# Adding the input in memory: output tiles turned into staging and accumulated by GpSimd's transfers, in a linear-attention and MLP block

## The chip, the cores and the metric

The kernel runs on one core of a Trainium2 chip, with one launch. The metric is the device time of one execution in microseconds; lower is better. Where several runs are shown, their median is used. Engines are called by their names: TensorE (PE, with its weight loads as PEld), VectorE (DVE), ScalarE (ACT), GpSimd (POOL) and SyncE (SP). SP, ACT and GpSimd can all issue DMA transfers, which run on the core's sixteen DMA engines.

## The reference

One input `x` of 2048 tokens by 512 features in float32 is normalised, and two blocks run on the same normalised tokens. Both are added to `x`:

```
xn  = layernorm(x)                       # no scale or bias
qkv = xn @ wqkv                          # 512 x 1536, 32 heads of 16
q, k = phi(q), phi(k)                    # phi(t) = (t+1 if t > 0 else exp(t)) + 1e-6
kv  = sum over tokens of k^T v,  z = sum over tokens of k
A   = ((q kv) / (q z + 1e-6)) @ wo       # 512 x 512
B   = relu(xn @ w1 + b1)^2 @ w2 + b2     # 512 x 1376, 1376 x 512
out = x + A + B
```

The last line is the one that matters here: the input, untouched, is added to the sum of both blocks before it is stored.

## The kernel before

**How the work is tiled.** The 2048 tokens are four blocks of 512 (`BT`); a block's result is held feature-major, so an output tile is 128 features by 512 tokens, and there are four of them per block (`TB = 4`), sixteen in all. Every float32 product is made of three passes over a rounded high part and a low part of each operand. The products of two token blocks at a time are done with Strassen's scheme, seven products for eight.

**Stages.** First, sixteen token tiles of 128 are loaded, normalised, transposed (the first eight by TensorE, the others by VectorE after thirty-two small transfers `xg<-xp` that regroup them) and multiplied by the key weights; the key-value sums grow on TensorE (`kx`). Behind the loop over tiles the values and the fused matrix of `wo` are made (`values`, `matrix`). Then a loop `for n in range(2)` handles two token blocks each: blocks t1 and t2 are 3 and 2 in the first pass, 1 and 0 in the second. A pass has an inner loop over pairs of weight columns `p` (two pairs for the attention's queries, seven for the MLP), whose results are kept in `rr` tiles, and then a list of jobs that multiply the squared or normalised rows with `w2` and the fused matrix. Operand tiles `ops` of the weights are spilled to memory (`wd`) in the first pass and loaded again later; eight buffers of them rotate.

**How an output tile leaves.** The result of a job stands in PSUM (`acc`, `ps`) or, in the second pass, partly in SBUF (`m1`, `m5`, `u2`), features by tokens. `add_turned` transposes it on VectorE in blocks of 32 by 32 into a scratch tile `o` and adds it with a second VectorE instruction to a staging tile `res`, which `load_res` has filled with the same block of `x` earlier: eight transfers of 128 KB, each for 32 partitions and with runs of 256 bytes. `store` writes the staging tile to the output in transfers of the same shape. The second half of the features of block t2 in the second pass is stored by SP and ACT in turn, and the very last tile is turned, added and stored in two parts (`PARTS`, `flush`).

**What sets the order.** The whole kernel is recorded first. `Program.add` collects the instructions with what they read and write; `Program.order` then gives every one a due time and plays the program up to 150 times with costs from `cost`, shifting due times where TensorE had to wait in the play, and keeps the best order. TensorE's own order is as recorded; the others (DVE, ACT, GpSimd, SP) take, at each moment, the ready instruction that is due first. The resulting instructions are emitted in that order, each engine's list is fixed, and an engine executes its list strictly in order. All profile rows of these instructions therefore carry one line, L301 (`emit`), and are told apart by tile names. A tile's buffer is named by its tag: `res` of the first pass takes the buffers `r3` (t1) and `r0` (t2), and in the second pass `slots_of` gives `r3` to the `rr` tile of pair 0 and `r0` to that of pair 5. The output tensor is kept out of the recorder's dependencies (`apart`), as nothing reads it. Transfers take one of eight semaphores in turn for SP and ACT together, so that each of them waits for the one eight before it; GpSimd's transfers have eight of their own.

L1568 reserves room for descriptors of GpSimd's transfers: `dynamic_dma_scratch_size=1024`, in bytes per partition. In the kernel before GpSimd issues no transfer.

Of the kernel before, what the change touches and what calls it, by code (L numbers as in the profile page):

```python
# [10 lines left out]
OP = mybir.AluOpType  # L11
# [63 lines left out]
class Program:  # L75
# [7 lines left out]
    def __init__(self, nc):  # L83
        self.nc = nc
        self.tasks = []
        self.seen = {}
        self.fixed = 0
        self.apart = None
        for e in ("tensor", "vector", "scalar", "gpsimd", "sync"):
            setattr(self, e, Recorder(self, e))  # L90
# [13 lines left out]
    def add(self, engine, name, args, kw):  # L104
# [7 lines left out]
        outs = [r for r in outs if r[0] != self.apart]  # L112
        t.preds, t.first = {}, []
        for regions, write in ((ins, False), (outs, True)):
            for r in regions:
                before = self.seen.get(r[0], [])
                hit = [(o, wrote) for q, o, wrote in before
                       if (write or wrote) and q[0] < r[2] and r[1] < q[1] and q[2] < r[4] and r[3] < q[3]]
                if isinstance(r[0], Place) and r[0].last and not hit:
                    t.first.append(r[0].last)  # L120
                for o, wrote in hit:
                    if o is not t:
                        t.preds[o.index] = max(t.preds.get(o.index, 0), 1 if wrote else 0)
# [11 lines left out]
    def cost(self, t, out, ins):  # L135
# [16 lines left out]
        elif t.engine == "vector":  # L152
            a, b = self.DVE.get(t.name, (0.1, 0.5))
            t.dur = a + src * b / 960
            t.lock = t.name in ("tensor_tensor", "scalar_tensor_tensor") and n > 64 and not any(map(in_psum, ins))
        elif t.engine == "gpsimd":
            t.dur = 0.2 + src * 2.3 / 1000 if t.name == "tensor_tensor" else 0.3
            t.lock = t.name == "tensor_tensor"
        else:
            b = 1  # L160
            for s, k in out.ap:
                b *= k
            run = 1
            for a in (out, *ins):
                d = list(a.ap)
                c = d[-1][1] if d[-1][0] == 1 else 1
                run = min(run, c) if run > 1 else c
            t.size, t.lag = 4 * b, 2.8 if b > P * P else 2.0
            t.dur = 0.43 if out.ap[0][1] == P and run >= 512 else 0.62 if ins and isinstance(ins[0], View) and isinstance(out, View) else 0.5
            t.size = t.size * max(1.0, (0.009 + run * 4 / 27e3) / (run * 4 / 24e3)) if run > 1 else b * 150  # L170
# [142 lines left out]
def kernel(  # L313
# [831 lines left out]
    for i in range(2, NT):  # L1145
# [29 lines left out]
        if i == 3:  # L1175
            advance()
        if i == 8:
            run(*[lambda j=j: piece_v(j) for j in range(NJ)])
# [66 lines left out]

    def load_res(t, pool, tag):
        r = pool.tile([P, 2, BT // 32, 64], F32, name=f"res{t}", tag=tag)
        for g, h, rows in out_blocks(xf, t):
            nc.sync.dma_start(r[g, h], rows)
        return r  # L1250

    def add_turned(r, c, src, part=slice(0, BT)):
# [5 lines left out]

    def store(r, t, *halves, by=None, blocks=slice(0, BT // 32)):
        for g, h, rows in out_blocks(of, t):  # L1260
            if h in halves:
                (by or nc.sync if g.start % 64 else nc.sync).dma_start(rows[:, blocks], r[g, h, blocks])

# [9 lines left out]
    for n in range(2):  # L1273
# [75 lines left out]
        for p in range(NK + 1):  # L1349
# [61 lines left out]
            if n == 0 and p == NK - 1:  # L1411
                res = {t1: load_res(t1, work, "r3")}

# [11 lines left out]
        if n == 0:  # L1425
# [8 lines left out]
            sums = sums_of(xT[t1 - 2], xT[t2 - 2])  # L1434
            outs = [lambda c=c: add_turned(res[t1], c, acc[c]) for c in range(TB)]
            outs.append(lambda: store(res[t1], t1, 0, 1))

            made_t = []

            def step(e):  # L1440
                if e == 10:
                    res[t2] = load_res(t2, work, "r0")
                if e > 5:
# [35 lines left out]
            for c in range(TB):  # L1479
                add_turned(res[t2], c, acc_2[c])  # L1480
            store(res[t2], t2, 0, 1)
            continue

        X, Z = acc[:2], acc[2:]
        res = {t1: load_res(t1, keep, "B0"), t2: load_res(t2, keep, "A0")}
        W, Y = ([bank(f"{u}{c}", loop_tag) for c in range(2)] for u in "WY")
# [13 lines left out]
        def turned_to(t, a, src):  # L1500
            for c in range(2):
                add_turned(res[t], a + c, src[c])

# [24 lines left out]
        jobs.append((lambda: hz[:, 0], lambda s: second_z([*Z, *Y], range(NJ), s)))  # L1528
        at_end(lambda: (add_to(o["m1"], Z), turned_to(t1, 0, o["m1"])))
        jobs += phase_jobs(X, 5)  # L1530
# [3 lines left out]
        jobs += phase_jobs(X, 6)  # L1534
        at_end(lambda: (add_to(o["m5"], X), turned_to(t2, 2, o["m5"]), store(res[t2], t2, 1, by=nc.scalar)))
        jobs += phase_jobs(Y, 3, False, True)
        at_end(lambda: (add_to(o["u2"], Y), turned_to(t1, 2, o["u2"]), store(res[t1], t1, 0, 1)))
        jobs.append((lambda: hz[:, 1], lambda s: second_z(X, range(2), s)))
# [3 lines left out]
        def flush(part):  # L1542
            add_turned(res[t2], 1, ends_in[part.start], part)
            store(res[t2], t2, 0, by=nc.scalar, blocks=slice(part.start // 32, part.stop // 32))

# [36 lines left out]
```

## Time and profile before

| | us |
|---|---|
| three runs | 410.43, 410.69, 410.69; median 410.69 |
| the profiled execution | 410.82 |
| its span, from the first to the last instruction | 409.1 |
| TensorE busy in it | 402.0 |
| VectorE busy in it | 338.8 |
| ScalarE busy in it | 264.4 |
| GpSimd busy in it | 28.3 |
| granted TensorE clock, mean | 0.997 |

The page gives the busy time of each engine, the span in forty slices, and the chain of work that ended last, followed back from the last instruction. The groups of instructions name output tile and input tile (`res<-o,res` is the add of a turned tile into staging), partitions by elements, a count, then busy time, the mean of one in ns and the idle time of the engine just before them with what ended it. The rows of DMA issues end with the median time from the issue to the landing of the data. A timeline row has the start, the duration, the engine and the instruction, with the idle time before it and what released it in brackets. A row of windows gives, for a stretch, its length, the busy time of PE, PEld, DVE, ACT and POOL with counts, the granted clock, the busy share of the DMA engines and GB/s.

### The profile page before, as it was taken

Reading aid. Unit: us, or ns where it says so; the run is one execution under the profiler, and the core shown is the slowest. Engines: PE = TensorE matmul, PEld = TensorE weight load, DVE = VectorE, ACT = ScalarE, POOL = GpSimd, SP = SyncE. Lnnn points to the kernel's source line nnn. Section 1 sums busy time; section 2 is a strip of 40 time slices with the busy share of each in tenths; the row PEclk is TensorE's granted clock in tenths of the full one; section 3 lists DMA queues with packets and bytes.
Section 4 is the critical chain, followed back from the end, with each engine's and each line's share of the span. In section 5 each row is a group of like instructions: output and inputs, shape, how many; then the busy total and the mean of one; then the engine's idle time right before and its main releaser. Section 6 shows DMA issues by size and latency. Waiting matters only on the chain.

```text
span 409.1 us, 5570 instructions
## 1 busy us (share of the span) xinstructions
PE 402.0 (98%) x1805; PEld 333.1 (81%) x1805; DVE 338.8 (83%) x578; ACT 264.4 (65%) x449; POOL 28.3 (7%) x48
## 2 busy tenths in 40 slices
PE   8999999999999999999999999999999999999994
PEld 7788888888888888888888888888888888888883
DVE  5899997989788699999989742799999999786794
ACT  5786666766867988889952421367888777545430
POOL 2233422220000000000000000000000000000000
PEclk9999999999999999999999999999999999999998
DMA  7863524933979779756799999999877789979424
GB/s 241 279 169 96 163 70 108 334 107 116 358 272 322 245 271 316 270 217 260 269 336 279 292 378 359 273 297 377 282 238 254 269 220 269 266 250 279 159 52 103
DMA packets 80497, 99.34 MB, mean 243 GB/s; under 512 B 40306, under 2 KB 51570, under 8 KB 80212
## 3 DMA queue, kind: packets, MB, share of 16 engines
q1 hardware_dynamic: 78324, 98.47, 75.0%
q10 hardware_dynamic: 2144, 0.52, 0.6%
q8 instruction: 14, 0.23, 0.2%
q14 instruction: 15, 0.12, 0.1%
HBM read 60.96 MB, written 35.92 MB: 237 GB/s over the span
## 4 chain that ended last, share of the span: by engine, by line
PE 98%; DVE 1%; ACT 0%; issue 0%
PE ps L301 53%; PE acc L301 44%; DVE res L301 0%; DVE o L301 0%; ACT xs1h L301 0%; DVE zb L301 0%; DVE odds L301 0%
## 5 line engine op out<-in xcount | busy, mean ns | idle before, releaser
L301 PE MATMUL ps<-s,ops 128*128 128x512 f32 x393 | 91.5, 389 | 0.0
L301 PEld LDWEIGHTS ps<-s,ops 128*128 128x128 f32 x393 | 73.8, 188 | 15.3
L301 PE MATMUL acc<-s,ops 128*128 128x512 f32 (+1 forms) x294 | 67.1, 382 | 0.0
L301 PEld LDWEIGHTS acc<-s,ops 128*128 128x128 f32 x294 | 54.1, 188 | 10.8
L301 PE MATMUL acc<-pk,tok 128*128 128x512 f32 x192 | 47.1, 394 | 0.0
L301 ACT ACTIVATE s<-rr 128x512 fp32r<-128x512 f32 x50 | 31.3, 632 | 21.7 <-DVE s L301 10.9
L301 PEld LDWEIGHTS acc<-pk,tok 128*128 128x128 f32 x192 | 35.4, 188 | 7.9 <-DVE pk L301 0.6
L301 DVE TENSOR_TENSOR s<-rr,s 128x512 fp32r<-128x512 f32 x50 | 34.1, 688 | 9.3 <-ACT s L301 8.2
L301 PE MATMUL ps<-T,ops 128*128 128x512 f32 x168 | 41.4, 390 | 0.0
L301 PE MATMUL acc<-T,ops 128*128 128x512 f32 x168 | 41.2, 389 | 0.0
L301 PEld LDWEIGHTS acc<-T,ops 128*128 128x128 f32 x168 | 31.5, 188 | 6.5
L301 PEld LDWEIGHTS ps<-T,ops 128*128 128x128 f32 x168 | 31.5, 188 | 6.5
L301 POOL TENSOR_TENSOR tok<-xp,tok 128x512 fp32r<-128x512 f32 x16 | 23.1, 1443 | 41.9 <-ACT tok L301 24.1
L301 PE MATMUL ps<-xs0h,ops 128*128 128x512 f32 x72 | 23.7, 389 | 0.0
L301 ACT ACTIVATE ops<-raw 128x512 fp32r<-128x512 f32 (+1 forms) x28 | 16.2, 591 | 4.3 <-PE ps L301 2.1
L301 DVE TENSOR_TENSOR ops<-raw,ops 128x512 fp32r<-128x512 f32 (+1 forms) x28 | 17.1, 617 | 1.6 <-ACT ops L301 1.5
L301 PE MATMUL acc<-xs0h,ops 128*128 128x512 f32 x56 | 18.4, 389 | 0.0
L301 ACT ACTIVATE s<-rf 128x512 fp32r<-128x512 f32 x10 | 6.3, 634 | 18.3 <-PE ps L301 16.2
L301 ACT ACTIVATE rr<-acc 128x512 f32<-128x512 f32 x23 | 13.5, 588 | 6.9 <-PE acc L301 6.7
L301 DVE TENSOR_TENSOR rr<-acc,rr 128x512 f32<-128x512 f32 x21 | 14.5, 691 | 3.8 <-PE acc L301 2.0
L301 ACT ACTIVATE k<-ps 128x512 f32<-128x512 f32 x16 | 9.6, 597 | 12.4 <-PE ps L301 12.3
L301 ACT ACTIVATE rr<-rr,odds 128x512 f32<-128x512 f32 x15 | 10.9, 723 | 7.9 <-DVE rr L301 7.8
(152 smaller groups left out, 753.3 us busy)
## 6 DMA issues: line engine op xcount, KB each, us to landing
wd<-ops SPq DMA_DIRECT2D x35, 512.0 KB, 4.2
ops<-wd SPq DMA_DIRECT2D x35, 512.0 KB, 5.7
ops<-wd SPq DMA_DIRECT2D x56, 256.0 KB, 4.4
wd<-made SPq DMA_DIRECT2D x14, 512.0 KB, 5.7
res<-in_A_x_dram SPq DMA_DIRECT2D x32, 128.0 KB, 5.6
out_dram<-res SPq DMA_DIRECT2D x26, 128.0 KB, 5.0
x<-in_A_x_dram SPq DMA_DIRECT2D x5, 512.0 KB, 5.2
raw<-in_B_w_dram SPq DMA_DIRECT2D x10, 256.0 KB, 4.7
```

Of the source, the lines that this page charges most:

```text
L301: getattr(getattr(self.nc, t.engine), t.name)(*map(real, t.args), **{k: real(a) for k, a in t.kw.items()})
```

## The change

Four transfers of 1 MB each, recorded in the loop over token tiles (`i` in 4, 6, 8, 10) and issued by SP, copy `x` to the output in memory. For twelve of the sixteen output tiles, counted in the code, nothing is loaded into the staging tile any more: `turned_in` transposes the result straight into it, with no add. These are all eight tiles of the first pass and, in the second pass, the two made of `m1` (block t1, first half) and the two made of `m5` (block t2, second half). `add_out` then issues, from GpSimd, transfers with `accum_op=OP.add`, which add the staging tile to what stands in the output. Each strip of 128 KB goes as two transfers of 64 KB (8 of the 16 blocks of 32 tokens each): sixteen transfers for a whole block, eight for half a block, 48 in all.

The other four tiles (the two made of `u2`, and the two last ones) still have `x` loaded into staging, are added there by VectorE, and are stored over the copy. Half of the strips of the `u2` tiles are now stored by GpSimd (two transfers of 128 KB), the others by SP; the last ones go by SP and ACT as before. The recorder lets every write from a staging tile to the output wait for the four copies (`laid`), and the planner's cost of issuing a transfer on GpSimd is set to 1.2 us. L301 and L1568 of the kernel before are L306 and L1586 in the changed one.

```
+        if len(given) == 2 and not isinstance(given[0][1], View) and given[0][1].tensor.name == self.apart:
+            if isinstance(given[1][1], View):
+                t.preds.update((o.index, 1) for o in self.laid)
+            else:
+                self.laid.append(t)
...
-            t.dur = 0.43 if out.ap[0][1] == P and run >= 512 else 0.62 if ins and isinstance(ins[0], View) and isinstance(out, View) else 0.5
+            t.dur = 0.43 if out.ap[0][1] == P and run >= 512 else 0.62 if ins and isinstance(ins[0], View) and isinstance(out, View) else 0.5 if t.engine != "gpsimd" else 1.2
...
+        if i in (4, 6, 8, 10):
+            rows = slice((i - 4) // 2 * BT, (i - 2) // 2 * BT)
+            nc.sync.dma_start(of[rows, :], xf[rows, :])
...
-    def load_res(t, pool, tag):
+    def res_of(t, pool, tag, *halves):
         r = pool.tile([P, 2, BT // 32, 64], F32, name=f"res{t}", tag=tag)
         for g, h, rows in out_blocks(xf, t):
-            nc.sync.dma_start(r[g, h], rows)
+            if h in halves:
+                nc.sync.dma_start(r[g, h], rows)
         return r
+
+    def turned_in(r, c, src):
+        nc.vector.transpose(r[:, c // 2].rearrange("p b (d c) -> p c b d", c=2)[:, c % 2], src)
...
-    def store(r, t, *halves, by=None, blocks=slice(0, BT // 32)):
+    def add_out(r, t, *halves):
         for g, h, rows in out_blocks(of, t):
             if h in halves:
-                (by or nc.sync if g.start % 64 else nc.sync).dma_start(rows[:, blocks], r[g, h, blocks])
+                for blocks in (slice(0, BT // 64), slice(BT // 64, BT // 32)):
+                    nc.gpsimd.dma_start(rows[:, blocks], r[g, h, blocks], accum_op=OP.add)
+
+    def store(r, t, half, blocks=slice(0, BT // 32), by=nc.scalar):
+        for g, h, rows in out_blocks(of, t):
+            if h == half:
+                (by if g.start % 64 else nc.sync).dma_start(rows[:, blocks], r[g, h, blocks])
...
-                res = {t1: load_res(t1, work, "r3")}
+                res = {t1: res_of(t1, work, "r3")}
...
-            outs = [lambda c=c: add_turned(res[t1], c, acc[c]) for c in range(TB)]
-            outs.append(lambda: store(res[t1], t1, 0, 1))
+            outs = [lambda c=c: turned_in(res[t1], c, acc[c]) for c in range(TB)]
+            outs.append(lambda: add_out(res[t1], t1, 0, 1))
...
-                add_turned(res[t2], c, acc_2[c])
-            store(res[t2], t2, 0, 1)
+                turned_in(res[t2], c, acc_2[c])
+            add_out(res[t2], t2, 0, 1)
...
-        res = {t1: load_res(t1, keep, "B0"), t2: load_res(t2, keep, "A0")}
+        res = {t1: res_of(t1, keep, "B0", 1), t2: res_of(t2, keep, "A0", 0)}
...
-                add_turned(res[t], a + c, src[c])
+                (add_turned if (t, a) == (t1, 2) else turned_in)(res[t], a + c, src[c])
...
-        at_end(lambda: (add_to(o["m1"], Z), turned_to(t1, 0, o["m1"])))
+        at_end(lambda: (add_to(o["m1"], Z), turned_to(t1, 0, o["m1"]), add_out(res[t1], t1, 0)))
...
-        at_end(lambda: (add_to(o["m5"], X), turned_to(t2, 2, o["m5"]), store(res[t2], t2, 1, by=nc.scalar)))
+        at_end(lambda: (add_to(o["m5"], X), turned_to(t2, 2, o["m5"]), add_out(res[t2], t2, 1)))
...
-        at_end(lambda: (add_to(o["u2"], Y), turned_to(t1, 2, o["u2"]), store(res[t1], t1, 0, 1)))
+        at_end(lambda: (add_to(o["u2"], Y), turned_to(t1, 2, o["u2"]), store(res[t1], t1, 1, by=nc.gpsimd)))
```

More of the change, by code (lines that the diff above doesn't have):

```diff
@@ L87, in __init__ @@
         self.fixed = 0
-        self.apart = None
+        self.apart, self.laid = None, []
         for e in ("tensor", "vector", "scalar", "gpsimd", "sync"):
@@ L155, in cost @@
             t.lock = t.name in ("tensor_tensor", "scalar_tensor_tensor") and n > 64 and not any(map(in_psum, ins))
-        elif t.engine == "gpsimd":
+        elif t.engine == "gpsimd" and t.name != "dma_start":
             t.dur = 0.2 + src * 2.3 / 1000 if t.name == "tensor_tensor" else 0.3
@@ L1441, in step @@
                 if e == 10:
-                    res[t2] = load_res(t2, work, "r0")
+                    res[t2] = res_of(t2, work, "r0")
                 if e > 5:
@@ L1543, in flush @@
             add_turned(res[t2], 1, ends_in[part.start], part)
-            store(res[t2], t2, 0, by=nc.scalar, blocks=slice(part.start // 32, part.stop // 32))
+            store(res[t2], t2, 0, slice(part.start // 32, part.stop // 32))
         at_end(lambda: run(lambda: add_turned(res[t2], 0, X[0]), *[lambda part=part: flush(part) for part in PARTS]))
```

## The prediction

> **What bounds the kernel now.** First the page: busy time, the slices, the chain by engine; then the chain in order of time.
>
> ```profile
> span 409.1 us, 5570 instructions
> ...
> PE 402.0 (98%) x1805; PEld 333.1 (81%) x1805; DVE 338.8 (83%) x578; ACT 264.4 (65%) x449; POOL 28.3 (7%) x48
> ...
> PE   8999999999999999999999999999999999999994
> ...
> POOL 2233422220000000000000000000000000000000
> ...
> DMA  7863524933979779756799999999877789979424
> GB/s 241 279 169 96 163 70 108 334 107 116 358 272 322 245 271 316 270 217 260 269 336 279 292 378 359 273 297 377 282 238 254 269 220 269 266 250 279 159 52 103
> ...
> PE 98%; DVE 1%; ACT 0%; issue 0%
> ```
> ```profile
> 392.30 8.85 PE ps L301 x39
> ...
> 401.17 0.73 DVE o L301
> ...
> 403.83 0.42 DVE res L301
> ```
>
> The chain that ended last is TensorE for 98% of the span: after the first microseconds it never waits until 401.15, and then VectorE turns and adds the last strips until 404.25. The DMA engines are nearly full in the middle (up to 378 GB/s); GpSimd is idle after a fifth of the span. So work taken from DVE, SP or ACT before 401 gains nothing by itself. What the change can do to the time is to make TensorE wait, or to alter the 8 us behind it.
>
> The profiled execution took 410.82 us, 1.7 us of it outside the span; the median of the runs shown is 410.69. The sums below start from 410.8.
>
> **What goes away.** The rows for the removed kinds (the last number of a DMA row is us from issue to landing):
>
> ```profile
> L301 DVE TENSOR_TENSOR res<-o,res 128x512 f32<-128x512 f32 x16 | 10.9, 686 | 0.2
> L301 DVE STREAM_TRANSPOSE o<-acc 128x512 f32<-128x512 f32 x4 | 2.8, 709 | 0.0
> L301 DVE STREAM_TRANSPOSE xT<-xg 128x512 f32<-128x512 f32 x8 | 5.6, 705 | 1.0 <-DMA xTd<-t 0.7 <-DMA xg<-xp 0.3
> ```
> ```profile
> L301 SPq DMA_DIRECT2D res<-in_A_x_dram x32: 320/486/2856, 75.0 to 350.4; - x32
> ```
> ```profile
> res<-in_A_x_dram SPq DMA_DIRECT2D x32, 128.0 KB, 5.6
> out_dram<-res SPq DMA_DIRECT2D x26, 128.0 KB, 5.0
> xT<-xTd SPq DMA_DIRECT2D x2, 1024.0 KB, 6.0
> out_dram<-res ACTq DMA_DIRECT2D x2, 128.0 KB, 2.7
> out_dram<-res SPq DMA_DIRECT2D x4, 64.0 KB, 1.8
> out_dram<-res ACTq DMA_DIRECT2D x4, 64.0 KB, 2.0
> ```
>
> By the code twelve of the sixteen 128x512 adds go (eight in the first pass, m1 and m5 in the second): 12 x 0.686 = 8.2 us of DVE. The transposes stay and write every second element of the staging tile; a transpose with strided operands took 705 ns against 709, so nothing is added. SP loses 24 of 32 loads and 24 of 30 stores, 48 x 0.486 = 23 us of issuing. All of it lies under TensorE: gain 0. In the changed program's order TensorE's instructions stand exactly as before; DVE's and ACT's are shuffled a little by the planner. I cost that at 0, under the same cover; without it a shifted DVE instruction costs about its own 0.7 us.
>
> In the tail something could be gained:
>
> ```profile
> 398.90 1.40 SPq L301 DMA_DIRECT2D out_dram<-res  x3
> ```
> ```profile
> 405.72 0.87 SPq L301 DMA_DIRECT2D out_dram<-res  x2
> ```
> ```profile
> SPq L301 <- DMA out_dram<-res: 1.8, 3, 1.4
> ```
>
> The last add ends at 404.25, but SP issues the last two stores only at 405.72, having waited 1.4 us for an earlier transfer (each SP or ACT transfer waits for the one eight before it). The change leaves 10 output stores on SP and ACT at the end instead of 16, so that wait can go: at most 1.4 us, if nothing else is later.
>
> **What is added early.** Four copies of 1 MB from x to the output, all standing right behind the b1 loads on SP.
>
> ```profile
> 22.20 1.03 SPq L301 DMA_DIRECT2D odds<-in_B_b_dram  x2
> ```
> ```profile
> 39.45 5.02 SPq L301 DMA_DIRECT2D xg<-xp  x8
> ```
> ```profile
> 48.63 0.71 DVE L301 STREAM_TRANSPOSE xT<-xg 128x512 f32<-128x512 f32 x1 [0.71 <-DMA xTd<-t]
> ...
> 49.37 0.63 ACT L301 ACTIVATE xs1h<-xT 128x512 fp32r<-128x512 f32 x1 [0.57 <-DVE xT L301]
> ...
> 52.36 0.19 PEld L301 LDWEIGHTS ps<-wkh,xs1h 128*128 128x128 f32 x1
> ```
> ```profile
> 26.00:35.00 9.00, 9.00 (x45) 7.45 (x44) 8.18 (x22) 7.33 (x17) 2.23 (x4) 1.00 0.20 61
> ```
>
> They go out from about 24 us, where the DMA engines are only 0.20 busy (next to last column). No copy from memory to memory is in the trace. Ends: 2.8 us each (1 MB at the fullest slices, 378 GB/s) and 6.0 (the 1 MB load of xT with its wait). I take 4, as both sides are long runs: done near 42. By the rule of eight the seventh xg transfer (39.45) waits for the fourth copy: 2.5 us late. The turned tile must reach TensorE at 52.36; it was ready at 50.0 (transpose ends 49.34, then one ACT pass of 0.63), which covers 2.4. So 0 here; at 6.0 a copy the last lands at 48, 8.6 us late, and TensorE would lose up to 6.
>
> **What is added late: GpSimd's queue.** 48 accumulating transfers of 64 KB (each strip in two halves) and two plain stores of 128 KB. None of this kind is in the trace. If they overlap freely, one costs its issue: at the low end SP's 0.486. If each waits for the one before, it costs issue plus landing: 1.8 us in the quiet tail and up to 5.6 for a 128 KB transfer in the busy middle. The issue on GpSimd is not shown either; the change's own planner charges 1.2. I take the serial reading: L1568 gives this queue's descriptors a room of only 1,024 bytes, and the code halves every accumulating strip while it leaves the plain stores of the same queue whole. That is an inference from code, so the other reading is a rival. Nearest row, quiet: 1.2 + 1.8 = 3.0 us each. Busy: 1.2 + 2.8 = 4.0, the 2.8 between 1.8 (same size, quiet) and 5.0 (twice the size, busy). The 128 KB store: 1.2 + 2.7 = 3.9. These are estimates from the rows.
>
> [...]
>
> Now who waits for them. The staging tiles of the first pass sit in buffers r3 and r0, which the second pass reuses for rr of pair 0 and pair 5:
>
> ```profile
> 216.96 0.71 DVE L301 STREAM_TRANSPOSE o<-acc 128x512 f32<-128x512 f32 x1
> ```
> ```profile
> 226.33 2.48 SPq L301 DMA_DIRECT2D out_dram<-res  x4
> ```
> ```profile
> 260.41 0.60 ACT L301 ACTIVATE rr<-acc 128x512 f32<-128x512 f32 x1 [5.74 <-PE acc L301]
> ```
> ```profile
> 261.57 2.88 PE L301 MATMUL acc<-T,ops 128*128 128x512 f32 x12
> ```
> ```profile
> 317.53 0.60 ACT L301 ACTIVATE rr<-acc 128x512 f32<-128x512 f32 x1
> ```
> ```profile
> 321.41 2.88 PE L301 MATMUL acc<-T,ops 128*128 128x512 f32 x12
> ```
> ```profile
> 200.00:240.00 40.00, 40.00 (x178) 33.14 (x177) 33.11 (x47) 18.79 (x28) 0.00 (x0) 1.00 1.04 301
> 240.00:270.00 30.00, 30.00 (x134) 24.82 (x134) 17.20 (x32) 9.64 (x16) 0.00 (x0) 1.00 0.97 334
> ...
> 380.00:390.00 10.00, 10.00 (x46) 8.29 (x45) 8.37 (x14) 4.83 (x8) 0.00 (x0) 1.00 0.37 128
> ```
>
> Before, the last store out of r3 was issued by 228.8 and landed long before ACT's copy at 260.41. In the changed program that copy of rr waits for the sixteen accumulations of the first strip, and everything queued behind it on ACT waits too. TensorE comes back to the copied bank in the second half of its 261.57 group (six matmuls later, at 262.9), so the copy may start at 262.3 without loss. The four transposes now run back to back and end at 216.96 + 4 x 0.71 = 219.8. From there to 262.3 at 4.0 us each, 10.6 transfers are done; TensorE then stands, the traffic dies down, and the other 5.4 take 3.0 each, until 278.4. **Stall: 16.1 us.** It vanishes if a transfer takes under 42.5 / 16 = 2.65 us.
>
> The next sixteen run from 278.4, at 3.5 (between the two) until 334.4. The copy into r0 stood at 317.53 and TensorE needs its bank at 322.77; shifted by the stall, 333.6 to 338.9. So 0 here, and 7 us if they take 4.0.
>
> In the tail:
>
> ```profile
> 365.05 0.70 DVE L301 STREAM_TRANSPOSE o<-m 128x512 f32<-128x512 f32 x1
> ```
> ```profile
> 388.17 0.70 DVE L301 STREAM_TRANSPOSE o<-m 128x512 f32<-128x512 f32 x1
> ```
>
> On the clock of before (all later by the stall): m1's eight accumulations are ready near 365 and take until 389; m5's eight, ready at 388, until 413; behind them in GpSimd's order stand the two plain stores, 2 x 3.9, until 420.8. SP's last landing (406.27 + 1.8 = 408.1) lay 1.0 before the end of the span, so the end is at 421.8 instead of 409.1: **12.7 us more**, and the 1.4 us that SP and ACT could save are hidden. Sum: 410.8 + 16.1 + 12.7 = 439.6, **439 us**.
>
> **The rivals.**
> 1. The transfers overlap (the other side: faster). GpSimd issues one per 1.2 us or less: r3 is free by 245, m5's eight are issued by 398, the stores, whose data is ready at 398.9, by 401.3, landed by 404. Then only the tail changes: 410.8 - 1.4 = 409.4. It decides where 8 transfers and 2 stores fit in 20 us, 2 us each. For it: SP's strips are issued every 0.5 to 0.7 us while they take 5.0 to land. Against: the small room.
> 2. Serial, but a transfer takes little more than a quiet ACT store of 64 KB, 2.0. No stall at r3; tail 388 + 8 x 2.0 + 2 x 2.7 + 1.0 = 410.4, +1.3: 412; at 2.5 (stores 3.3) 388 + 20 + 6.6 + 1.0 = 415.6: 417. [...]
> 3. Serial and slow, 4.5 throughout the busy part: 219.8 + 72 = 291.8, stall 29.5; the next sixteen end at 363.8 against 322.2 + 29.5, another 12.1; with the tail's 12.7 the time is 465.
> 4. The early copies make TensorE wait too: up to +6 on any of these; alone 417.
>
> **How the numbers follow.** Forecast 0.58 (422 to 451: 2.9 throughout and 2.6 in the tail, to 4.3 busy and 3.4 quiet); rival 1 0.11; rival 2 0.15; rival 3 0.12; rival 4 alone or nothing measurable 0.04. The range 412 to 468 leaves out rival 1 and what lies above rival 3. Runs of before differ by 0.06%, and 0.2% is about what can be told from no change: faster 0.12 (rival 1 and a little), same 0.03, slower 0.85.
>
> **What would show it.** Right: ACT's first rr copy waits for a DMA into the output, TensorE idles once for 5 to 30 us near 262, GpSimd's transfers stand 3 to 4 us apart with DMA as releaser, and the last landing is GpSimd's. Wrong: transfers 1.2 us apart; no idle at 262; the last work on SP or ACT; or idle time near 52.

## The result, and the profile after

The changed kernel takes 480.62 us (median, 478.77 to 482.85) where the kernel before takes 410.65 (410.43 to 410.90): a ratio of 1.1711, 95% interval 1.1694 to 1.1729. The forecast was slower, 439 us, and it was short by 42 us; rival 3 with its 465 came nearer, and the range ended at 468. The profiled execution took 480.73 us, 478.8 of it in the span.

The page of the changed kernel: span, busy time, three rows of the span in 40 slices, and the chain by engine.

```profile
span 478.8 us, 5575 instructions
...
PE 406.5 (85%) x1805; PEld 335.0 (70%) x1805; DVE 329.5 (69%) x566; ACT 263.7 (55%) x449; POOL 74.8 (16%) x98
...
PE   8999999999999999999999005999962999999700
...
POOL 2332232100000000001111232211121000112322
PEclk9999999999999999999999556999995999999955
...
PE 55%; issue 22%; DVE 6%; POOL 6%; DMA 5%; ACT 4%; SPq 1%; POOLq 0%; DVEq 0%; ACTq 0%
```

(The helper through which every instruction goes is L306 here and L301 before.) TensorE's work is about the same (406.5 us busy against 402.0), but its row now has two holes and an empty end, the granted clock falls to half in the same places, and the chain is TensorE for 55% only. The next 22% are "issue", time for which the profile names no releaser; it lies between GpSimd's transfers. Who waits is in the view of waits (us in total, times, longest):

```profile
POOL out_dram L306 <- issue: 156.9, 46, 7.9
...
ACT rr L306 <- DMA out_dram<-res: 62.4, 2, 44.3
...
PE acc L306 <- ACT rr L306: 42.5, 2, 29.1
```

ACT waits twice for a transfer into the output, TensorE waits twice for ACT. The timeline of ACT, then of TensorE, puts both waits at the copies of rr into r3 and into r0, as foreseen (first number the start, second the duration, in brackets the idle time before it):

```profile
291.65 0.60 ACT L306 ACTIVATE rr<-acc 128x512 f32<-128x512 f32 x1 [44.30 <-DMA out_dram<-res]
367.20 0.60 ACT L306 ACTIVATE rr<-acc 128x512 f32<-128x512 f32 x1 [18.11 <-DMA out_dram<-res]
```
```profile
292.30 2.93 PE L306 MATMUL acc<-T,ops 128*128 128x512 f32 x6 [29.08 <-ACT rr L306]
...
297.07 0.39 PE L306 MATMUL ps<-xs0h,ops 128*128 128x512 f32 x1
...
367.85 2.93 PE L306 MATMUL acc<-T,ops 128*128 128x512 f32 x6 [13.45 <-ACT rr L306]
...
374.88 0.40 PE L306 MATMUL acc<-T,ops 128*128 128x512 f32 x1
```

Why they wait so long is in GpSimd's own timeline. Of its fifty transfers, these are the first of each set, the last of most of them, and the places where the distance changes:

```profile
219.34 1.11 POOL L306 DMA_DIRECT2D out_dram<-res  x1 [35.67 <-DVE res L306]
...
262.22 0.96 POOL L306 DMA_DIRECT2D out_dram<-res  x1 [3.75 <-issue]
267.26 0.94 POOL L306 DMA_DIRECT2D out_dram<-res  x1 [4.08 <-issue]
...
288.88 0.95 POOL L306 DMA_DIRECT2D out_dram<-res  x1 [2.10 <-issue]
291.86 0.94 POOL L306 DMA_DIRECT2D out_dram<-res  x1 [2.04 <-issue]
...
352.38 0.95 POOL L306 DMA_DIRECT2D out_dram<-res  x1 [5.71 <-issue]
...
364.33 0.94 POOL L306 DMA_DIRECT2D out_dram<-res  x1 [2.00 <-issue]
412.85 0.94 POOL L306 DMA_DIRECT2D out_dram<-res  x1 [47.58 <-DVE res L306]
...
445.91 0.96 POOL L306 DMA_DIRECT2D out_dram<-res  x1 [2.17 <-DVE o L306]
...
472.42 0.69 POOL L306 DMA_DIRECT2D out_dram<-res  x1 [2.16 <-issue]
475.23 0.66 POOL L306 DMA_DIRECT2D out_dram<-res  x1 [2.11 <-issue]
```

An accumulation is issued in 0.95 us, and then GpSimd stands until the transfer has landed: by the landing times in the trace, 48 of the 49 transfers that follow another start 0.26 to 0.34 us behind the landing of the one before (the 49th, at 412.85, had to wait for m1's result). The trace counts a landing from the start of its issue, so the distance from one to the next is the landing, issue included, and these 0.3 us. From 219.34 to 262.22, with TensorE running, lie seven intervals, 6.1 us each; from 267.26 to 288.88, with TensorE standing, seven of 3.1. The sixteen of the second block (t2, buffer r0) are 4.8 apart: eleven intervals of 5.5 up to 352.38, then four of 3.0, in which TensorE stands again. Counted to the first of the next set, m1's eight are 4.1 apart and m5's eight 3.3. The table by stage shows what differs (last three columns: granted clock, share of time in which the DMA engines are busy, GB/s):

```profile
219.30:262.00 42.70, 42.70 (x190) 35.36 (x189) 22.46 (x40) 10.76 (x17) 6.79 (x7) 1.00 1.01 323
268.00:291.00 23.00, 0.00 (x0) 0.00 (x0) 0.00 (x0) 0.00 (x0) 6.84 (x8) 0.50 0.34 22
...
412.00:446.00 34.00, 34.00 (x152) 28.15 (x151) 24.07 (x37) 16.59 (x27) 7.66 (x9) 1.00 0.68 160
```
```profile
292.00:297.00 5.00, 4.70 (x12) 3.74 (x13) 2.74 (x5) 3.74 (x7) 1.75 (x2) 0.56 0.61 146
297.00:300.00 3.00, 3.00 (x14) 2.47 (x14) 2.63 (x5) 0.86 (x3) 0.50 (x1) 1.00 0.76 225
...
368.00:372.00 4.00, 4.00 (x11) 3.13 (x12) 3.86 (x7) 3.70 (x7) 0.00 (x0) 0.56 0.02 6
```

The second fence holds the two restarts: after each stall TensorE runs at half its clock for some four microseconds (in windows of 1 us the clock is 0.50 up to 296 and up to 371, and 1.00 from 297 and from 372 on; the 0.56 are means over both parts). At 0.227 us a matmul (39 in 8.85 in the chain of before) the twelve from 292.30 to 297.07 would take 2.72 us and took 4.77; the eighteen from 367.85 to 374.88 would take 4.08 and took 7.03, 0.55 of that being small waits.

So the 69.7 us of longer span are: first stall 29.1, its restart 2.05, second stall 13.45, its restart 2.95, and a longer end. The transpose that began at 401.17 before begins at 449.22; from there to the end of the span were 7.93 us and are 29.58, 21.65 more. What comes ahead of the first stall, the early copies with it, costs 0.1: TensorE's group of 261.57 stands at 261.69. Sum 69.3; 0.4 is not assigned.

### The profile page after: what moved, and what is told of

It reads as the page before. It is cut to its first block, busy times and chain, and to the rows that moved or that the text cites. A ratio compares the mean times of both kernels' runs of the same rounds, so it can differ in the third digit from the quotient of the medians.

```text
span 478.8 us, 5575 instructions
## 1 busy us (share of the span) xinstructions
PE 406.5 (85%) x1805; PEld 335.0 (70%) x1805; DVE 329.5 (69%) x566; ACT 263.7 (55%) x449; POOL 74.8 (16%) x98
## 3 DMA queue, kind: packets, MB, share of 16 engines
q10 hardware_dynamic: 1088, 0.26, 0.3%
## 4 chain that ended last, share of the span: by engine, by line
PE 55%; issue 22%; DVE 6%; POOL 6%; DMA 5%; ACT 4%; SPq 1%; POOLq 0%; DVEq 0%; ACTq 0%
PE ps L306 28%; PE acc L306 27%; POOL out_dram L306 6%; DVE s L306 3%; DMA xTd<-t 3%; ACT s L306 2%; DMA out_dram<-res 1%; SPq L306 1%; DVE rr L306 1%; ACT rr L306 1%; DMA xg<-xp 1%; DMA x<-in_A_x_dram 1%; DVE res L306 1%; DVE T L306 0%; DVE st L306 0%
## 5 line engine op out<-in xcount | busy, mean ns | idle before, releaser
L306 PE MATMUL ps<-s,ops 128*128 128x512 f32 x393 | 91.9, 390 | 0.5 <-ACT s L306 0.3
L306 POOL DMA_DIRECT2D out_dram<-res x50 | 47.0, 940 | 245.2 <-issue 156.9
L306 PEld LDWEIGHTS ps<-s,ops 128*128 128x128 f32 x393 | 73.6, 188 | 16.6 <-ACT s L306 0.8
L306 PE MATMUL acc<-T,ops 128*128 128x512 f32 x168 | 44.3, 408 | 42.5 <-ACT rr L306 42.5
L306 PEld LDWEIGHTS acc<-T,ops 128*128 128x128 f32 x168 | 32.9, 197 | 50.3 <-ACT rr L306 43.4
L306 PE MATMUL acc<-s,ops 128*128 128x512 f32 (+1 forms) x294 | 67.1, 382 | 0.0
L306 PEld LDWEIGHTS acc<-s,ops 128*128 128x128 f32 x294 | 54.1, 188 | 10.8
L306 DVE TENSOR_TENSOR rr<-acc,rr 128x512 f32<-128x512 f32 x21 | 14.5, 690 | 54.0 <-ACT rr L306 50.1
L306 ACT ACTIVATE rr<-acc 128x512 f32<-128x512 f32 x23 | 13.6, 590 | 67.7 <-DMA out_dram<-res 62.4
L306 PE MATMUL acc<-pk,tok 128*128 128x512 f32 x192 | 47.3, 394 | 0.1
L306 ACT ACTIVATE s<-rr 128x512 fp32r<-128x512 f32 x50 | 31.3, 630 | 20.3 <-DVE s L306 13.8
L306 DVE TENSOR_TENSOR s<-rr,s 128x512 fp32r<-128x512 f32 x50 | 34.2, 688 | 12.0 <-ACT s L306 11.1
L306 PE MATMUL ps<-T,ops 128*128 128x512 f32 x168 | 41.4, 390 | 0.0
L306 PEld LDWEIGHTS acc<-pk,tok 128*128 128x128 f32 x192 | 35.4, 188 | 8.3 <-DVE pk L306 1.0
L306 PEld LDWEIGHTS ps<-T,ops 128*128 128x128 f32 x168 | 31.5, 188 | 6.5
L306 POOL TENSOR_TENSOR tok<-xp,tok 128x512 fp32r<-128x512 f32 x16 | 22.9, 1435 | 40.7 <-ACT tok L306 28.3
L306 PE MATMUL ps<-xs0h,ops 128*128 128x512 f32 x72 | 23.7, 389 | 0.0
L306 ACT ACTIVATE ops<-raw 128x512 fp32r<-128x512 f32 (+1 forms) x28 | 16.3, 591 | 4.4 <-PE ps L306 2.2
L306 PE MATMUL acc<-xs0h,ops 128*128 128x512 f32 x56 | 18.4, 389 | 0.0
L306 DVE TENSOR_TENSOR ops<-raw,ops 128x512 fp32r<-128x512 f32 (+1 forms) x28 | 17.1, 618 | 1.6 <-ACT ops L306 1.5
L306 ACT ACTIVATE s<-rf 128x512 fp32r<-128x512 f32 x10 | 6.3, 633 | 17.5 <-PE ps L306 15.4
L306 POOL MEMSET raw_z<- 128x128 f32 (+1 forms) x2 | 0.7, 363 | 94.6 <-DMA wd<-ops 94.6
```

Source lines behind the costliest of these rows:

```text
L306: getattr(getattr(self.nc, t.engine), t.name)(*map(real, t.args), **{k: real(a) for k, a in t.kw.items()})
```

## The experiments

The kernel before, run beside each set, took 410.5 to 410.62 us; the ratios are against those runs.

### The price by itself: `price` and `price_wide`

A program with no layer in it issues only GpSimd's transfers, in sets: alone, as plain stores, beside SP's loads, beside VectorE's adds. The second differs in one number.

```diff
-    nc = _bacc.Bacc("TRN2", target_bir_lowering=False, num_devices=1, dynamic_dma_scratch_size=1024)
+    nc = _bacc.Bacc("TRN2", target_bir_lowering=False, num_devices=1, dynamic_dma_scratch_size=4096)
```

> None of the layer is computed: the four copies of x, then GpSimd's transfers by themselves: 16 accumulations of 64 KB with nothing beside them, 16 plain stores of 64 KB, 32 accumulations beside a stream of 64 loads of 512 KB from SP (it ends before they do), 16 accumulations beside VectorE adds 128x512 and no other transfer. Theory room (the descriptors' room of 1,024 bytes holds one accumulation, so each waits for the one before to land): alone 3.0 us apart, beside the loads 5 to 6.5 and 3.0 again once the loads are through, beside VectorE 3.0; plain stores, with half the descriptors, clearly closer, 1.0 to 1.6. Theory accumulation (accumulations follow one another by nature): the same here but for nothing that this run tells. Theory path (whatever GpSimd issues is serial): plain stores 3.0 as well. Theory VectorE (its adds slow GpSimd's descriptor writing, and that was the busy price): 4 or more beside the adds, 3.0 beside the loads.

> The same program with a room of 4,096 bytes instead of 1,024, nothing of the layer computed. Theory room: accumulations alone go down to the issue, 0.95 to 1.2 us apart; beside the loads 1 to 2. Theory accumulation or path: 3.0 alone and 5 to 6.5 beside the loads, as with the small room.

GpSimd's timeline of `price`, then of `price_wide` (several issues close together are one row, with their count):

```profile
24.11 0.94 POOL L42 DMA_DIRECT2D out_dram<-alone  x1 [2.17 <-issue]
...
61.02 0.94 POOL L42 DMA_DIRECT2D out_dram<-alone  x1 [1.98 <-issue]
...
64.97 0.95 POOL L44 DMA_DIRECT2D out_dram<-alone  x1
...
79.25 1.16 POOL L44 DMA_DIRECT2D out_dram<-alone  x2 [0.57 <-issue]
...
95.30 0.95 POOL L42 DMA_DIRECT2D out_dram<-alone  x1 [7.15 <-issue]
...
168.29 0.94 POOL L42 DMA_DIRECT2D out_dram<-alone  x1 [7.04 <-issue]
```
```profile
16.67 15.52 POOL L42 DMA_DIRECT2D out_dram<-alone  x16 [16.23 <-DMA alone<-in_A_x_dram]
28.64 12.77 POOL L44 DMA_DIRECT2D out_dram<-alone  x16
...
53.15 0.93 POOL L42 DMA_DIRECT2D out_dram<-alone  x1 [2.10 <-issue]
...
115.91 0.94 POOL L42 DMA_DIRECT2D out_dram<-alone  x1 [2.37 <-issue]
```

us from one transfer to the next (first to last start over the number of intervals; for a row of 16, its length over 16):

| 64 KB by GpSimd | room 1,024 | room 4,096 |
|---|---|---|
| accumulation, alone | 3.08 (12 intervals) | 0.97 (x16) |
| plain store, alone | 0.96 (x16, 64.97 to 80.41) | 0.80 (x16) |
| accumulation beside loads of 512 KB | 8.11 (9 intervals) | 2.99 (21 intervals) |
| accumulation beside VectorE's adds | 3.07 (218.54 to 279.89, 20 intervals) | |

Only the room differs, so the room makes the accumulations serial: theory "room" holds, "accumulation" and "path" fall (with four times the room the same accumulations go out at the speed of the issue). VectorE's adds cost them nothing (3.07 us against 3.08). Beside loads one at a time takes 8.1 us, more than the 5 to 6.5 expected, and in the large room 2.99, more than the 1 to 2 expected.

### In the kernel: `two_fit` and `plain`

`two_fit` is the changed kernel with `dynamic_dma_scratch_size=1088`; `plain` drops the accumulation, so that x is missing from twelve of the sixteen output tiles:

```diff
-                    nc.gpsimd.dma_start(rows[:, blocks], r[g, h, blocks], accum_op=OP.add)
+                    nc.gpsimd.dma_start(rows[:, blocks], r[g, h, blocks])
```

> The changed kernel with a room of 1,088 bytes in place of 1,024, the most that SBUF has left. [...] Theory accumulation or path: nothing changes, 480.

> The changed kernel with the 48 accumulations turned into plain stores of the same 64 KB by GpSimd (x is left out of twelve of the sixteen tiles). [...] Theory path: 465 to 480.

`two_fit` took 422.42 us (1.0298, 1.0263 to 1.0334), `plain` 411.36 (1.0024, 1.0012 to 1.0036). Sixty-four bytes of room take 58 us off. That two accumulations would fit in 1,088 bytes was an estimate of mine; with two the spacing halves, from 6.1 us to 3.05 beside the traffic, and I gave 411 to 418 us. In `two_fit` GpSimd has issued 14 transfers by 263.28, 3.4 us apart on average. Many accumulations now leave in pairs, as in this row of GpSimd's timeline; TensorE's timeline has one stall left:

```profile
267.35 1.92 POOL L306 DMA_DIRECT2D out_dram<-res  x2 [3.12 <-issue]
```
```profile
271.88 2.93 PE L306 MATMUL acc<-T,ops 128*128 128x512 f32 x6 [8.65 <-ACT rr L306]
```

The end is as before: its chain has the transpose at 411.89 and the span ends at 420.2, 8.3 us later. `two_fit` is 4 us over that range since 3.4 is not 3.05, and the restart's slow clock was left out again. `plain` shows no stall, and also no gain: it lacks all the loads and adds of the twelve tiles and still isn't below the kernel before.

The landing times in the traces tell how many transfers the room holds. Where GpSimd stands, its next issue begins some 0.3 us behind the landing of an earlier transfer. With a room of 1,024 bytes and accumulations of 64 KB that is the one before (all 95 in `price_rows` further down). In `two_fit` it is the second before (35 of 37 waits), in `plain` the third before (27 of 32), in `price_wide`, beside the loads, the seventh before (19 of 23). So an accumulation of 64 KB takes about half of the 1,024 bytes: two don't fit in them, and do in 1,088.

### The parts: `first_only` and `second_only`

Each keeps the four copies and uses accumulation in one pass, with load, add and store as before in the other. The core of `first_only` (`second_only` reverts the first pass in the same way):

```diff
-        res = {t1: res_of(t1, keep, "B0", 1), t2: res_of(t2, keep, "A0", 0)}
+        res = {t1: res_of(t1, keep, "B0", 0, 1), t2: res_of(t2, keep, "A0", 0, 1)}
...
-                (add_turned if (t, a) == (t1, 2) else turned_in)(res[t], a + c, src[c])
+                add_turned(res[t], a + c, src[c])
...
-        at_end(lambda: (add_to(o["m1"], Z), turned_to(t1, 0, o["m1"]), add_out(res[t1], t1, 0)))
+        at_end(lambda: (add_to(o["m1"], Z), turned_to(t1, 0, o["m1"])))
...
-        at_end(lambda: (add_to(o["m5"], X), turned_to(t2, 2, o["m5"]), add_out(res[t2], t2, 1)))
+        at_end(lambda: (add_to(o["m5"], X), turned_to(t2, 2, o["m5"]), store(res[t2], t2, 1, by=nc.scalar)))
...
-        at_end(lambda: (add_to(o["u2"], Y), turned_to(t1, 2, o["u2"]), store(res[t1], t1, 1, by=nc.gpsimd)))
+        at_end(lambda: (add_to(o["u2"], Y), turned_to(t1, 2, o["u2"]), store(res[t1], t1, 0, 1)))
```

> The copies and the first pass as in the changed kernel (32 accumulations), the second pass as before: its strips are loaded, added on VectorE and stored by SP and ACT. Theory parts (the 70 us are two stalls with their slow clock, 48, and a longer tail, 21.65, which do not depend on each other): 410.8 + 48 = 458 to 460 us, both stalls at their places. Theory chain (the tail is long only because the stalls push work together, or the stalls only because of the second pass's share of the queue): clearly off that, 445 or less, or 475 and more.

> The copies and the second pass as in the changed kernel (16 accumulations and GpSimd's stores of u2's odd strips), the first pass as before. Theory parts: no stall, tail as in the changed kernel, 410.8 + 21.65 = 432 to 433 us. Theory chain: without the stalls the transfers beside m1 find less traffic and take 3.0 each, tail 12.7 as I had it: 423 to 424.

`first_only` took 459.38 us (1.1188, 1.1172 to 1.1204), 48.8 more than before; `second_only` 430.87 (1.0497, 1.0476 to 1.0517), 20.25 more. Together 69.0 of the changed kernel's 70.0: the parts add up (`second_only` came out 1 us under the 432 to 433 expected). TensorE's timeline of `first_only` has both stalls at their places and sizes:

```profile
291.71 2.93 PE L306 MATMUL acc<-T,ops 128*128 128x512 f32 x6 [28.50 <-ACT rr L306]
...
368.37 2.93 PE L306 MATMUL acc<-T,ops 128*128 128x512 f32 x6 [14.04 <-ACT rr L306]
```

GpSimd's timeline of `second_only`, where nothing stalls:

```profile
365.01 1.12 POOL L306 DMA_DIRECT2D out_dram<-res  x1 [181.24 <-DVE res L306]
...
397.17 0.94 POOL L306 DMA_DIRECT2D out_dram<-res  x1 [2.16 <-DVE s L306]
...
421.94 0.68 POOL L306 DMA_DIRECT2D out_dram<-res  x1 [2.02 <-issue]
```

m1's eight are 4.0 us apart and m5's 3.1. So the long end does not come of the stalls: m1's eight are slow with stalls before them and without, beside the loads for TensorE's last stages (160 GB/s between 412 and 446 in the changed kernel).

### Which buffer: `swap`

```diff
-                t = four(f"rr{n}_{k}", f"r{((0, 2), (3, 2, 1, 4, 5, 0))[n][k]}")
+                t = four(f"rr{n}_{k}", f"r{((0, 2), (2, 1, 4, 5, 3, 0))[n][k]}")
```

> The changed kernel with the buffers of the second pass in another order, (2, 1, 4, 5, 3, 0) for (3, 2, 1, 4, 5, 0): r3 is reused for pair 4, whose first copy stood at 305 before, instead of pair 0's at 260. Theory queue (32 accumulations have to go through one by one before r0 is written, whatever buffer comes first): the first stall goes or shrinks to under 10 us, the one at r0 grows to 35 to 48, sum as before: 470 to 484 us. Theory buffer (r3's early reuse alone costs the 31 us of the first stall and its slow clock): about 449.

It took 480.82 us (1.1719, 1.1667 to 1.1770), as the changed kernel. TensorE's timeline:

```profile
313.75 2.73 PE L306 MATMUL acc<-T,ops 128*128 128x512 f32 x6 [3.00 <-ACT rr L306]
...
367.66 2.93 PE L306 MATMUL acc<-T,ops 128*128 128x512 f32 x6 [37.99 <-ACT rr L306]
```

The stalls are now 3.0 and 38.0, 41.0 in sum, against 29.1 and 13.45, 42.5. The buffer decides where TensorE waits; how long is decided by 32 transfers that go through one at a time ahead of r0.

### Smaller pieces: `quarters`

```diff
-                for blocks in (slice(0, BT // 64), slice(BT // 64, BT // 32)):
+                for blocks in [slice(b, b + 4) for b in range(0, BT // 32, 4)]:
```

> The changed kernel with each strip accumulated in four transfers of 32 KB instead of two of 64 KB, 96 in all, room still 1,024 bytes. [...] Theory fixed cost (each accumulation takes some 3 us whatever its size, one after the other): 96 at 3 to 5, over 550 us.

436.00 us (1.0614, 1.0599 to 1.0629): 44.6 below the changed kernel, though the same bytes go in twice as many transfers, so theory "fixed cost" falls. My estimate was 420 to 432 us, with three pieces in the room, 2.0 us per 32 KB beside the traffic and a first stall of 11; that three would fit was not shown then. It is 4 us over: 22 of the first 32 were issued by 264, 2.0 us per 32 KB, but the next three took until 273 before the fast quiet set in, and TensorE stood 17.2 us. Where GpSimd stands here, it goes on behind the landing of the third transfer before (47 of 51 waits): three of these halves fit in 1,024 bytes.

### What was removed, and the copies: `removed` and `copies_only`

`copies_only` is the kernel before with the four copies. `removed` turns the twelve tiles straight into staging and stores them by SP, so that x is missing from them:

```diff
-        if i in (4, 6, 8, 10):
-            rows = slice((i - 4) // 2 * BT, (i - 2) // 2 * BT)
-            nc.sync.dma_start(of[rows, :], xf[rows, :])
...
-                for blocks in (slice(0, BT // 64), slice(BT // 64, BT // 32)):
-                    nc.gpsimd.dma_start(rows[:, blocks], r[g, h, blocks], accum_op=OP.add)
+                nc.sync.dma_start(rows, r[g, h])
```

> The kernel before with the four copies of 1 MB from x to the output alone; every strip is loaded, added on VectorE and stored over them as before. If the copies are hidden, as I counted them: 410.6, within 0.2%. If TensorE waits for the turned x tiles behind them (rival 4): up to 416.

> What the change takes away, alone: twelve strips are turned straight into staging and stored by SP, without load and add (x is left out of them), no copies and no accumulations; GpSimd keeps the two stores of u2's odd strips. If the removed adds, loads and issues lie under TensorE: 410.6, at best 409.3 with SP's wait of 1.4 us at the end gone. If they were worth their own time (8.2 us of VectorE): 402 to 405.

`copies_only` took 410.87 us (1.0015, 1.0006 to 1.0024), `removed` 411.44 (1.0025, 1.0015 to 1.0035). The copies are hidden but for some 0.4 us. What the change takes away is worth nothing; `removed` is even 0.9 us slower, and what costs that is not shown. SP's wait at the end is still in it (SP issues its last two stores from 405.82, against 405.72 before), so the 409.3 could not come.

### SP's wait at the end: `early_half` and `early_half_act`

The kernel before, with m1's strips stored when m1 is done; the second also gives u2's odd strips to ACT.

```diff
-        at_end(lambda: (add_to(o["m1"], Z), turned_to(t1, 0, o["m1"])))
+        at_end(lambda: (add_to(o["m1"], Z), turned_to(t1, 0, o["m1"]), store(res[t1], t1, 0)))
...
-        at_end(lambda: (add_to(o["u2"], Y), turned_to(t1, 2, o["u2"]), store(res[t1], t1, 0, 1)))
+        at_end(lambda: (add_to(o["u2"], Y), turned_to(t1, 2, o["u2"]), store(res[t1], t1, 1, by=nc.scalar)))
```

> The kernel before with the store of m1's four strips moved up to where m1 is done, near 366, instead of beside u2's at 398.9; so SP issues eight transfers at the end instead of twelve, and its last two need not wait 1.4 us for an earlier one. If that wait sets the end: 409.2 to 409.6. If the landings of the last strips set it whatever SP does: 410.6.

> The same, and u2's two odd strips stored by ACT instead of SP, which leaves SP six transfers at the end. If issues on SP set the end: 408.6 to 409.3, a little below the other; if ACT's issues then wait for each other before the last parts: 410 or more.

`early_half` changed nothing (410.60; 1.0003, 0.9994 to 1.0012): the planner orders by readiness, not by where a line stands, and had these stores at 367 already. SP's timeline of the kernel before:

```profile
367.12 0.34 SPq L301 DMA_DIRECT2D out_dram<-res  x1
368.70 1.65 SPq L301 DMA_DIRECT2D out_dram<-res  x3
```

So this run tells nothing of the wait. `early_half_act` took 410.07 (0.9991, 0.9982 to 0.9999). SP's waits behind 395 for a transfer into the output are gone there (one of 2.5 us, ahead of the issue at 393, stands in both kernels), and the time fell by about 0.4 us, not 1.4. ACT's share of the stores changed with it, so the 0.4 can't be put down to the wait alone. It is the fastest kernel of the study, by less than the 0.2% that a measurement can tell.

### What sets the price beside traffic: `price_rows` and `price_small`

Accumulations one at a time beside five streams of loads; `price_small` halves the accumulation and the room.

```diff
-        to_out(r, 0, 2, True)
+        to_out(r, 0, 4, True)
...
-    nc = _bacc.Bacc("TRN2", target_bir_lowering=False, num_devices=1, dynamic_dma_scratch_size=1024)
+    nc = _bacc.Bacc("TRN2", target_bir_lowering=False, num_devices=1, dynamic_dma_scratch_size=512)
```

> None of the layer is computed. 16 accumulations of 64 KB, one at a time by the room of 1,024 bytes, alone and then beside five streams of loads by SP: 512 KB in rows of 4 KB, 512 KB in pieces of 1 KB, 128 KB in rows of 1 KB, 256 KB in rows of 2 KB, 1 MB in rows of 8 KB (the loads sum to 16 to 25 MB each). [...] Theory share (bytes share the bandwidth): some 8 beside all. [...]

> The same streams, with accumulations of 32 KB and a room of 512 bytes, in which again only one fits; nothing of the layer is computed. [...] Alone 2.5 to 3.0 in any case.

Starts of `price_rows` on GpSimd's timeline, first and last of the set beside rows of 4 KB and of the set beside rows of 8 KB, six and five intervals apart; the others are read in the same way:

```profile
75.38 0.95 POOL L46 DMA_DIRECT2D out_dram<-alone  x1 [6.28 <-issue]
...
124.16 0.95 POOL L46 DMA_DIRECT2D out_dram<-alone  x1 [7.34 <-issue]
...
432.25 0.95 POOL L46 DMA_DIRECT2D out_dram<-alone  x1 [9.29 <-issue]
...
483.04 0.94 POOL L46 DMA_DIRECT2D out_dram<-alone  x1 [9.36 <-issue]
```

| beside | 64 KB: us apart, added | 32 KB: us apart, added |
|---|---|---|
| nothing | 3.10 | 2.80 |
| 128 KB loads, rows of 1 KB | 4.85, 1.75 | 4.47, 1.67 |
| 512 KB loads, pieces of 1 KB | 6.89, 3.79 | 6.10, 3.30 |
| 256 KB loads, rows of 2 KB | 7.05, 3.95 | 5.84, 3.04 |
| 512 KB loads, rows of 4 KB | 8.13, 5.03 | 6.64, 3.84 |
| 1 MB loads, rows of 8 KB | 10.16, 7.06 | 7.50, 4.70 |

A share by bytes, some 8 us beside all, does not fit: beside the loads the 64 KB accumulations are 4.85 to 10.16 apart. Two other estimates of mine from these rows don't fit either. If the added time followed the size of the loads' pieces, the 5.03 beside rows of 4 KB would be a quarter, 1.26, beside pieces of 1 KB, 4.4 apart, and would halve with the accumulation; if it followed the bytes queued ahead, the pieces of 1 KB would give 8.1 like the rows, and half the accumulation would change nothing. Measured are 6.89 beside the pieces of 1 KB, and an added time that falls by a third or less when the accumulation halves, and grows with the size of the loads and with that of their elements: as if there were a part per piece and a part that each transfer pays once. From two sizes the split can't be shown, and the mechanism stays open.

## Why the prediction fell short, step by step

- **Serial transfers, because of the room: right.** Inferred from one constant in the code; `price` against `price_wide`, `two_fit` and the landing times now show it. How much of the room a transfer takes was an estimate of mine. The runs show that two accumulations of 64 KB fit in 1,088 bytes and not in 1,024, and of plain stores, 0.96 us apart in `price`, three in 1,024 and not four (`plain`). If nothing else stands in the room, an accumulation takes more than 512 and at most 544 bytes, a plain store more than 256 and at most 341, 0.47 to 0.67 of it. No run counts descriptors; the half that `price` was expected to show for plain stores is seen only as this share of the room.
- **The quiet price, 3.0: right by luck** (measured 2.95 to 3.1). The sum was 1.2 of issue and behind it 1.8 of landing, the landing of a plain store. But the trace counts a landing from the start of its issue: in `price` the accumulations alone land in 2.8 us, the issue of 0.95 included, and are 3.08 apart. So the sum counted an issue twice, and took a landing that was 1.0 too short; the two errors nearly cancel. GpSimd's plain stores of 64 KB do land in 2.2 (median), near the 2.0 of rival 2, but accumulations follow each other at 3.1 alone and more beside traffic, so that rival is out.
- **The busy price, 4.0: wrong, and this step carries most of the error.** It took a landing of 2.8, nearer a quiet store of the same size than a busy one of twice the size. Measured were 6.1 us per transfer in the first stretch, a landing of 5.8 on average. With that in the prediction's own sum, 42.5 / 6.1 = 7 are done by 262.3 and nine remain at 3.1: a stall of 28 us, against 16.1 foretold and 29.1 measured. The row for the busy 128 KB store had the better sign: beside traffic a transfer's own bytes count for little (with half the bytes, `price_small` saves a third of the added time or less).
- **The second wait, "0 here, and 7 us if they take 4.0": wrong for the same reason.** It rests on 3.5 per transfer; measured were 4.8 on average, 5.5 while TensorE runs, and the wait was 13.45. The 7 doesn't follow from the prediction's own numbers either: at 4.0 the sixteen end at 342.4, against 338.3 for ACT's copy, 4 us late.
- **The tail, 12.7: the same price again, 21.65.** It took the quiet 3.0 for m1's eight, although loads for TensorE run beside them: they took 33.1 us, not 24, so m5's could start only at 445.91 although its transposes ended at 435.57. m5's took 26.5 instead of 24. The plain stores, at 2.8, were cheaper than the 3.9 I gave them.
- **Left out: the clock after a stall.** The sum counted a stall at its length. Each restart cost 2 to 3 us more, 5.0 in sum. The granted clock falls to 0.50 some 2.5 us into the first stall and 3.5 into the second, and stays there until 4.1 and 3.7 us after TensorE starts again.
- **The error in sum.** First stall 13.0, second wait 13.45, tail 8.95, restarts 5.0: 40.4 of the 41 us that the forecast was short, and all but the restarts come of the price beside traffic.
- **What was removed, 0: right** (`removed`, `plain`). **The early copies, 0: right** within 0.4 us, and rival 4 is out. The last copy landed at 40.7 (foretold: near 42), the seventh xg transfer was issued 1.25 us late, at 40.70, and the weight load of 52.36 stands at 52.48. One copy lands 12.0 us after its issue, but they overlap: the four together take 16.7. **The tail wait of 1.4 us "that can go"**: in the changed kernel it went, hidden as foretold; in `early_half_act`, without GpSimd's stores in the way, 0.4 came of it.
- **Rival 3** (4.5 throughout, 465) had the mechanism with a price nearer the truth. I gave it 0.12. That its stall of 29.5 meets the 29.1 is a coincidence: 4.5 is the mean of the first sixteen, made of 6.1 beside traffic and 3.1 without. Neither it nor the forecast's own band went above 4.5, though the upper bound that I had named myself, an issue and a landing of 5.6, makes 6.8 (5.9 with the issue counted once): the range used the middle of the bounds, not their end.
- **The signs.** ACT's wait for a DMA into the output and GpSimd's last landing came as written. TensorE stood twice, not once, the transfers were 3.1 to 6.1 us apart, not 3 to 4, and the profile names "issue" as GpSimd's releaser, not a DMA.

## What to carry to other kernels

When transfers of a queue go one at a time, price them by what the DMA engines carry beside them, and take the range beyond the busiest landing in the trace: the longest median of a 64 or 128 KB transfer was 5.6 here, and the same accumulation cost 3.1 us alone and 4.9 to 10.2 beside streams of loads. Where a view counts a landing from the start of its issue, don't add the issue to it. Before work is moved to GpSimd's accumulating transfers, see how many fit in their queue's room: here 64 bytes more were worth 58 us. And work that lay under TensorE was worth nothing when removed (`removed`, 411.44 us, 1.0025), while its replacement brought TensorE to a stand twice, which cost the stalls, 42.5 us, and then each time about four microseconds at a granted clock of 0.50.

## What the runs showed that was not expected

- A room of 1,088 bytes instead of 1,024 takes the changed kernel from 480.6 to 422.4 us, though VectorE, ACT and SP do the same work.
- More in flight raises the throughput beside traffic as well: 2.99 us per accumulation in the large room, with seven in flight, against 8.11 one at a time, beside the same loads.
- Accumulations of half the size are hardly faster one at a time: 2.80 us against 3.10 alone.
- The four copies of 1 MB within memory overlap. Each lands 12.0 us after its issue in the kernel (median) and 9.4 with little beside them, all four within 16.7 and 14.7, and they cost the kernel about 0.4 us.
